# One gate-weight load in place of four, and a re-planned start, in a four-layer attention and GLU kernel

## Chip, core and metric

The kernel runs on one core of one Trainium2 chip. The metric is the device time of one execution in microseconds, lower is better. Times of a profiled execution are read from its trace, counted from the first instruction.

## What is computed

2048 tokens of width 448 pass through four residual layers: local dilated attention (A), gated bilinear MLP (B), A, B. Cut from the reference:

```python
x = A_x
x = x + _A_ref(_layernorm(x), A_wqkv, A_wo)                 # layer 0
x = x + _B_ref(_layernorm(x), B_w_gate, B_w_up, B_w_down)   # layer 1
x = x + _A_ref(_layernorm(x), A_wqkv, A_wo)                 # layer 2
x = x + _B_ref(_layernorm(x), B_w_gate, B_w_up, B_w_down)   # layer 3

def _A_ref(x, wqkv, wo):        # 16 heads of 28; each token looks at 8 tokens, 2 apart
    q, k, v = ...               # x @ wqkv
    logits = einsum("bhsd,bhswd->bhsw", q, kg) * scale
    attn = softmax(where(mask, logits, -1e9))
    return einsum("bhsw,bhswd->bhsd", attn, vg) @ wo

def _B_ref(x, w_gate, w_up, w_down):
    return einsum("bsf,fd->bsd", (x @ w_gate) * (x @ w_up), w_down)   # F = 1792
```

All data are bfloat16.

## The kernel before

Even and odd tokens are separated, so that the dilated window becomes a band of neighbours. The tokens lie in 16 blocks of 128, and each layer works on chunks of 256 or 512 tokens. `SEQ` gives the order of the jobs: `A00` is layer 0, chunk 0; `B10` layer 1, chunk 0; attention chunks and MLP chunks of the next layer alternate.

For each chunk `ln_chunk` normalises blocks on DVE and ACT (statistics `st` L582, `mv` L584, logarithm and exponential for `rstd` L585 and L587, normalised `xn_sb` L603). The normalised block is transposed into `xnTa` or `xnTb`: in layer 0, chunks 0 to 2, by TensorE against an identity (L612, copied out at L618); in all other chunks by a DMA transpose on SP's queue (L606). In layer 0 chunk 3 is blocks 10 to 13 and chunk 4 blocks 14 and 15.

Attention: `qk_chunk` multiplies by the query and key weights `WQK` (L650, four units of 14 matmuls in a chunk; a unit's key half has the key `Kps`, its query half `Qps`), evicts to `qk` (L702), and sends a few rows of it to DRAM (L711, "PW"), from where they come back transposed (L722). `v_group` makes V with `WV` (L650 too). For each block of 120 queries there are scores (L793), exponentials (L800), masks (L806), denominators (L820 early, by shuffles later) and the product with V (L826); `y_blocks` multiplies by `wo_g` (L666). MLP: `b_chunk` multiplies by gate and up weights (L907), evicts gate (L913), multiplies (L916, `hT`) and applies the down weights `WD` (L666, and L928 for the last two blocks).

The weights and x are loaded at the start, all through `plain_dma` (L464), on two queues. SP's queue has in this order: x blocks 0 to 3 (two loads), two of the four staged parts of wqkv, x blocks 4 to 7, the V weights, x blocks 8 to 11, x blocks 12 to 15, four parts of wo, and the up weights. ACT's queue has the other two staged parts, four loads of a quarter of the gate weights each, and two halves of the down weights. x, wqkv and the down weights fill 128 partitions with rows of 448 numbers or twice that. Gate weights go to partitions 0 to 63 of `WGU` and up weights to partitions 64 to 127; an up row has 1792 numbers, a row of a gate quarter 448. An instruction that issues a DMA stands in its engine's program order: on ACT it comes between activations and waits there for what it depends on.

The order on each engine is not written by hand. Every step is an `Op` with a duration, dependencies and a priority; `Sched.schedule` plays the program through with those durations and picks, engine by engine, the ready op of least priority. The loads take part with due times after their issue (`XL`, `WVL`, `STL`, `BL`, `WOL`, and the numbers called `lat`); these are planning numbers and cause no wait on the chip. Priorities come from `HEAD_P` (normalisation of the first chunks), `PR` (by kind of step) and `JP` (by job). `HOLD_BB` says how long the planner keeps a step of another matmul tiling waiting. At run time each engine follows its list and waits on semaphores for what it depends on. The list of one engine is strictly in order: an instruction that waits holds up all behind it. Before the real work TensorE runs 48 matmuls on zeros (L515).

Of the kernel before, what the change touches and what calls it, by code (L numbers as in the profile page):

```python
# [17 lines left out]
NCH = S // 512  # L18
# [8 lines left out]
MAIN = "R64"  # L27
PE_T = ('00', '01', '02')
HEAD_LN = 5
HEAD_P = (-32.97, -30.35, -18.21, -18.15, -16.4)  # L30
HOLD_A = 0.0
HOLD_BA = 2000.0
HOLD_BB = 500.0
HOLD_N = 3
D_PE = 1
DPARTS = ((0, 7), (7, 14))
# [8 lines left out]
AVC = True  # L45
AVC_E = ("act", "dve")
NBK = 8
PR = {'E': 5.21, 'lnv': 1.44, 'N': 2.25, 'S': 1.29, 'H': -17.16, 'VT': -3.79, 'QK': 2.58, 'G': 5.11, 'R': -15.24, 'Tps': 23.39, 'Ddps': -6.83, 'V': 1.75, 'Yps': -9.35, 'rstd': 0.76, 'Rs': -4.41, 'Rl': -5.78, 'mv': -8.05, 'Ex': -1.78, 'Oc': 6.12, 'QKps': -0.5, 'x': -0.56, 'Gps': 9.84, 'PW': -4.56, 'bn': 0.52, 'xn': -0.08, 'T': -7.71, 'AV': 1.69, 'VVps': 0.13}
JP = {'A04': 1.75, 'B32': 97.25, 'B33': -8.83, 'A00': -4.95, 'B12': 1.14, 'A22': 1.53, 'B10': -7.93, 'B14': 0.49, 'B13': 1.25, 'A21': -4.76, 'B11': 6.29, 'B31': 0.68, 'B34': -7.33, 'A01': -0.41, 'A23': 0.99, 'A02': 0.46, 'A20': -20.09, 'B30': 0.88, 'A03': 0.17}
XL = (2700.0, 2700.0, 5500.0, 8000.0, 10000.0)  # L50
WVL = 6500.0
STL = (3300.0, 4300.0, 3500.0, 4600.0)
BL = (9000.0, 15000.0, 12000.0)
WOL = 11000.0
PLAIN = 4
ACH = {0: (256, 512, 512, 512, 256), 2: (512, 512, 512, 512)}
BCH = {1: (256, 512, 512, 512, 256), 3: (256, 512, 512, 512, 256)}
WARM = 18
FILL = 30
SEED = 768  # L60
JITTER = 0
ATT_P = -0.09
A_CAP = 5
B_CAP = 8
SEQ = "A00 A01 B10 A02 B11 A03 A04 B12 A20 B13 A21 B14 B30 A22 B31 A23 B32 B33 B34".split()
# [339 lines left out]
def build(nc, A_x, A_wqkv, A_wo, B_w_gate, B_w_up, B_w_down, out):  # L405
# [41 lines left out]
    sc = Sched()  # L447
    LAST = sc
    sem_names = ["pe", "act", "dve", "pool"]
    sem_names += [f"d_x{i}" for i in range(NCH)] + ["d_stg0", "d_stg1", "d_stg2", "d_stg3", "d_wv", "d_wo", "d_wg0", "d_wg1", "d_wg2", "d_wg3", "d_wu", "d_wd0", "d_wd1", "d_out", "d_out2"]  # L450
    sem_names += ["d_x0h"]
    sem_names += [f"d_t{li}_{j}" for li in range(4) for j in range(len(CH[li]))]
    sem_names += [f"d_p{li}_{j}" for li in (0, 2) for j in range(len(CH[li]))] + [f"d_v{q}" for q in range(NQB)] + ["d_one0", "d_one2", "d_stv"]
# [9 lines left out]
    def plain_dma(q, dst, src, key, sem, deps=(), lat=3000.0, prio=0.0):  # L463
        sc.add(q, one(lambda E: E.dma_start(dst, src), key), {"sp": 520.0, "act": 500.0, "pool": 1000.0}[q], deps=deps, dma=sem, mode=0, lat=lat, prio=prio)  # L464
# [78 lines left out]
        src = A_wo.rearrange("(c j e) d -> j e c d", c=4, j=4, e=DH)[j]  # L543
        plain_dma("sp", dst, src, ("wo", j), "d_wo", deps=["c_wo"], lat=WOL, prio=-45)
    plain_dma("sp", WGU[64:128, :, :], B_w_up.rearrange("(k p) f -> p k f", p=64), "wu", "d_wu", lat=BL[1], prio=-44)
    for n in range(4):
        f0, f1 = n * F // 4, (n + 1) * F // 4
        plain_dma("act", WGU[0:64, :, f0:f1], B_w_gate[:, f0:f1].rearrange("(k p) f -> p k f", p=64), ("wg", n), f"d_wg{n}", lat=BL[0], deps=[("rstd", 0, 3)] * (n > 1), prio=-57 if n < 2 else -20)
    for n in range(2):
        plain_dma("act", WD[:, 7 * n:7 * n + 7, :], B_w_down[F // 2 * n:F // 2 * n + F // 2, :].rearrange("(c p) e -> p c e", p=128), ("wd", n), f"d_wd{n}", deps=[("rstd", 0, 7)], lat=BL[2], prio=-19)  # L550
    WDR = [("wd", 0), ("wd", 1)]
    WO = [("wo", j) for j in range(4)]

# [18 lines left out]
    def ln_chunk(li, j, prio):  # L572
        par = li % 2
        X = xnT[par]
        by_pe = f"{li}{j}" in PE_T
        t0, t1 = CH[li][j]
        blocks = range(t0 // 128, t1 // 128)
        groups = (1,) * len(blocks) if (li, j) == (0, 0) else (2,) * (len(blocks) // 2) + (1,) * (len(blocks) % 2)
        B0 = t0 // 128
        for n in groups:  # L580
            for B in range(B0, B0 + n):
                sc.add("dve", one(lambda E, B=B: E.bn_stats(st6[:, B, :], x_sb[:, B, :]), ("bn", li, B)), 525.0,  # L582
                       deps=[("x", li - 1, B)] + ([("xn", li - 1, B)] if li else []), prio=prio)
                sc.add("dve", one(lambda E, B=B: E.bn_aggr(mv[:, B, :], st6[:, B, :]), ("mv", li, B)), 100.0, deps=[("bn", li, B)], prio=prio - 0.1)  # L584
            sc.add("act", one(lambda E, B0=B0, n=n: E.activation(lnv[:, B0:B0 + n].unsqueeze(2), mv[:, B0:B0 + n, 1:2], ACT.Ln, bias=eps_sb[:, 0:1], scale=1.0), ("lnv", li, B0)),  # L585
                   190.0, deps=[("mv", li, B) for B in range(B0, B0 + n)] + ["c_eps"], prio=prio)
            sc.add("act", one(lambda E, B0=B0, n=n: E.activation(rstd[:, B0:B0 + n], lnv[:, B0:B0 + n], ACT.Exp, scale=-0.5), [("rstd", li, B) for B in range(B0, B0 + n)]),  # L587
                   165.0, deps=[("lnv", li, B0)], prio=prio)
            B0 += n
        for B in blocks:  # L590
            slot, prev = ring("xn", ("T", li, B) if not by_pe else ("Tps", li, B))
            if par == 0:
                src = _dup_view(x_sb[:, B, 0:256])
                dst = xn_sb[:, slot, 0:512].rearrange("p (a n) -> p a n", a=2)
                c0 = 128 * B
# [7 lines left out]
            sc.add("dve", one(lambda E, B=B, dst=dst, src=src: E.tensor_scalar(dst, src, mv[:, B, 0:1], rstd[:, B:B + 1], ALU.subtract, ALU.mult), ("xn", li, B)),  # L603
                   325.0 if par == 0 else 540.0, deps=[("rstd", li, B), ("mv", li, B), ("x", li - 1, B), prev], prio=prio - 0.2)
            if not by_pe:
                sc.add("sp", one(lambda E, slot=slot, c0=c0: E.dma_start_transpose(X[:, :, c0:c0 + 128], xn_sb[:, slot, 0:128 * nt]), ("T", li, B)),  # L606
                       1300.0, deps=[("xn", li, B)] + war, dma=f"d_t{li}_{j}", mode=0, lat=1400.0 if par == 0 else 1900.0, prio=prio)
            else:
                bk = Banks(1)
                ins = []  # L610
                for c in range(4):
                    ins.append((lambda E, c=c, slot=slot, bk=bk: E.transpose(ps[:, bk[0], :].bitcast(bf)[:, 128 * c:128 * (c + 1)], xn_sb[:, slot, 128 * c:128 * (c + 1)], ident[:]),  # L612
                                ("Tps", li, B) if c == 3 else None))
# [56 lines left out]
    def qk_chunk(li, j, prio):  # L670
# [37 lines left out]
        for b, w in [(b, w) for b in range(4) for w in range(2) if b + w < 4 and (li, j) != (0, 0)]:  # L708
            src = qk[32 * b + DH:32 * b + 32, w, :, c0:c1]
            dst = vt_dram[li].rearrange("(t w b r) n -> r w b t n", w=2, b=4, r=4)[:, w, b, :, c0:c1]  # L710
            sc.add("sp", one(lambda E, dst=dst, src=src: E.dma_start(dst, src), ("PW", li, j) if b == 3 else None), 550.0, deps=[("QK", li, j, c) for c in range(4)], dma=f"d_p{li}_{j}", mode=0, lat=3500.0 if li == 0 and j == 1 else 2200.0, prio=prio - 0.2)  # L711

    vslot, v2slot = {}, {}

    def vt_load(li, qb, prio):
        if li == 0 and qb < PLAIN:
            return
        k0, nk, _, _ = qb_info(qb)
        slot, prev = ring("v2", ("AV", li, qb))
        v2slot[(li, qb)] = slot  # L720
        deps = [("PW", li, j) for j in chunks_of(li, k0, k0 + nk)] + [("vones", li), prev]
        sc.add("sp", one(lambda E: E.dma_start_transpose(v2_sb[:, slot, :], vt_dram[li][:, k0:k0 + 128]), ("VT", li, qb)), 1300.0, deps=deps, dma=f"d_v{qb}", mode=li, lat=2500.0 if li == 0 and k0 < 768 else 1500.0, prio=prio)  # L722

    def v_group(li, qbs, prio):
        X = xnT[0]
# [161 lines left out]
    def b_chunk(li, j, n_b, prio):  # L887
# [173 lines left out]
```

## Time and profile before

| | |
|---|---|
| median of 6 runs | 406.39 us (405.11 to 407.6) |
| profiled execution | 406.44 us, its span 404.7 us, mean granted TensorE clock 0.987 |
| TensorE busy | 390.3 us (96%) |
| DVE / ACT / POOL busy | 292.7 / 222.9 / 15.5 us |
| DMA | 23.34 MB moved, 8.54 MB of it read from HBM by loads |

"Busy" is the time in which an engine had at least one instruction in work. "PE" is TensorE's matmul side, "PEld" its weight loads. A slice of the page's rows is a fortieth of the span, 10.1 us; "PEclk" is the clock that TensorE was granted, in tenths of full speed. In a view of waits a line names the engine that stood idle and what ended its idling; in a chain the pieces follow each other in time. The 1.7 us between span and time lie around the traced instructions.

### The profile page before, as it was taken

To read this page: it belongs to the slowest core of one execution; us is meant where nothing else is said; L and a number is where in the kernel's file an instruction comes from. 1 tells how busy PE (TensorE), PEld (TensorE's weight loads), DVE (VectorE), ACT (ScalarE), POOL (GpSimd) and SP (SyncE) were. 2 spreads that over 40 slices of the span, in tenths; PEclk is the share of its full clock that TensorE was granted. 3 is DMA by queue.
4 is the path that set the end of the run, shared out by engine and by line. 5 is a ranking of instruction groups with operands and counts; after the bars stand their busy time and mean duration, and the time that the engine had idled before them with its cause. 6 is when DMAs were issued, how large, how long until landed. Compare 5 with 4: busy or idle time off the path is not lost.

```text
span 404.7 us, 11727 instructions
## 1 busy us (share of the span) xinstructions
PE 390.3 (96%) x5046; PEld 212.6 (53%) x5046; DVE 292.7 (72%) x602; ACT 222.9 (55%) x406; POOL 15.5 (4%) x29
## 2 busy tenths in 40 slices
PE   8797899999999999999999999999999999999996
PEld 6443358644454444545455666844445455444584
DVE  5698398989997978687678965945784777674152
ACT  4596378676763955565564655625661575343040
POOL 6043000000000000000000000000000000000000
PEclk9899699999999999999999999999999999999999
DMA  8999141334024112222111205031030300320010
GB/s 232 271 214 213 32 59 29 62 54 64 14 47 68 33 28 46 47 28 39 15 24 25 51 16 101 20 61 43 11 45 26 70 0 3 84 55 2 13 36 24
DMA packets 58563, 23.34 MB, mean 58 GB/s; under 512 B 48112, under 2 KB 58032, under 8 KB 58512
## 3 DMA queue, kind: packets, MB, share of 16 engines
q1 hardware_dynamic: 54400, 18.86, 25.4%
q10 hardware_dynamic: 4112, 3.73, 4.0%
q8 instruction: 40, 0.66, 0.7%
q14 instruction: 11, 0.09, 0.1%
HBM read 8.54 MB, written 2.83 MB: 28 GB/s over the span
## 4 chain that ended last, share of the span: by engine, by line
PE 88%; DMA 4%; DVE 4%; ACT 1%; issue 1%; SPq 0%
PE ps L907 41%; PE ps L666 26%; PE ps L650 14%; DMA x_sb<-in_A_x_dram 2%; PE ps L826 2%; PE ps L793 2%; DMA xnTa<-xn_sb 2%; PE ps L928 1%; DVE st L582 1%; ACT E_sb L800 1%; DVE E_sb L806 1%; DVE x_sb L878 1%; PE ps L612 1%; DVE qk L702 0%; SPq L464 0%
## 5 line engine op out<-in xcount | busy, mean ns | idle before, releaser
L907 PE MATMUL ps<-xnTb,WGU 64*128 64x512 bf16 (+1 forms) x1960 | 179.4, 333 | 1.9 <-DVE R_sb L842 0.6
L907 PEld LDWEIGHTS ps<-xnTb,WGU 64*128 64x128 bf16 x1960 | 96.7, 94 | 73.0 <-issue 2.2
L913 ACT ACTIVATE g_sb<-ps 128x512 bf16<-128x512 f32 (+1 forms) x140 | 71.2, 513 | 92.7 <-PE ps L907 91.6
L916 DVE TENSOR_TENSOR hT<-g_sb,ps 128x512 bf16<-128x512 bf16 (+1 forms) x140 | 78.9, 575 | 44.8 <-ACT g_sb L913 42.1
L666 PE MATMUL ps<-WD,hT 64*128 64x448 bf16 x840 | 85.3, 349 | 0.2
L800 ACT ACTIVATE E_sb<-ps 128x960 bf16<-128x960 f32 (+1 forms) x68 | 63.0, 972 | 12.5 <-PE ps L793 12.4
L650 PE MATMUL ps<-xnTa,WQK 64*128 64x512 bf16 (+1 forms) x504 | 55.0, 362 | 5.2 <-DMA xnTa<-xn_sb 4.0
L666 PEld LDWEIGHTS ps<-WD,hT 64*128 64x128 bf16 x840 | 39.8, 94 | 37.2 <-PE ps L666 1.1
L878 DVE TENSOR_TENSOR x_sb<-x_sb,ps 128x448 bf16<-128x448 bf16 x62 | 35.9, 614 | 16.1 <-PE ps L666 16.0
L806 DVE TENSOR_TENSOR E_sb<-E_sb,MK 128x960 bf16<-128x960 bf16 (+1 forms) x64 | 43.5, 694 | 5.6 <-ACT E_sb L800 5.5
L582 DVE BATCH_NORM_STATS2 st<-x_sb 128x6 f32<-128x448 bf16 x64 | 37.3, 615 | 4.8 <-DMA x_sb<-in_A_x_dram 4.8
L650 PEld LDWEIGHTS ps<-xnTa,WQK 64*128 64x128 bf16 x504 | 24.1, 96 | 28.9 <-issue 6.5
L603 DVE TENSOR_SCALAR xn_sb<-x_sb,mv,rstd 128x512 bf16<-128x512 bf16 (+1 forms) x64 | 34.0, 573 | 1.3 <-ACT rstd L587 1.1
L666 PE MATMUL ps<-wo_g,oT 64*128 64x448 bf16 x256 | 29.6, 350 | 0.0
L702 ACT ACTIVATE qk<-ps 128x1024 bf16<-128x1024 f32 (+1 forms) x22 | 19.6, 906 | 16.6 <-PE ps L650 16.6
L702 DVE CAST qk<-ps 128x1024 bf16<-128x1024 f32 (+1 forms) x14 | 16.0, 1142 | 11.7 <-PE ps L650 11.5
L650 PE MATMUL ps<-WV,xnTa 64*128 64x336 bf16 (+2 forms) x252 | 23.9, 311 | 0.1
L844 ACT ACTIVATE R_sb<-R_sb 128x480 f32<-128x480 f32 (+1 forms) x30 | 18.0, 603 | 10.2 <-DVE R_sb L842 9.8
L860 DVE TENSOR_TENSOR oT<-O_sb,R_sb 128x480 bf16<-128x480 f32 (+3 forms) x32 | 19.5, 614 | 2.6 <-ACT R_sb L846 2.5
L846 ACT ACTIVATE R_sb<-R_sb 128x480 f32<-128x480 f32 (+1 forms) x34 | 20.4, 603 | 0.5
L842 DVE STREAM_SHUFFLE R_sb<-O_sb 128x480 f32<-128x480 f32 (+1 forms) x30 | 20.5, 689 | 0.0
L585 ACT ACTIVATE lnv<-mv,eps_sb 128x2 f32<-128x2 f32 (+1 forms) x33 | 9.6, 294 | 17.7 <-DVE mv L584 17.7
(55 smaller groups left out, 181.0 us busy)
## 6 DMA issues: line engine op xcount, KB each, us to landing
out_dram<-x_sb SPq DMA_DIRECT2D x15, 112.0 KB, 1.7
WGU<-in_B_w_gate_dram ACTq DMA_DIRECT2D x4, 392.0 KB, 10.2
WGU<-in_B_w_up_dram SPq DMA_DIRECT2D x1, 1568.0 KB, 20.3
WD<-in_B_w_down_dram ACTq DMA_DIRECT2D x2, 784.0 KB, 19.2
x_sb<-in_A_x_dram SPq DMA_DIRECT2D x3, 448.0 KB, 11.3
vt<-qk SPq DMA_DIRECT2D x49, 16.0 KB
xnTb<-xn_sb SPq DMA_TRANSPOSE x32, 3.0
v_sb<-vt SPq DMA_TRANSPOSE x30, 2.3
```

The lines of the kernel that those rows point to most:

```text
L582: sc.add("dve", one(lambda E, B=B: E.bn_stats(st6[:, B, :], x_sb[:, B, :]), ("bn", li, B)), 525.0, deps=[("x", li - 1, B)] + ([("xn", li - ...
L603: sc.add("dve", one(lambda E, B=B, dst=dst, src=src: E.tensor_scalar(dst, src, mv[:, B, 0:1], rstd[:, B:B + 1], ALU.subtract, ALU.mult), ( ...
L650: parts[0 if s < 3 else 1][1].append((lambda E, w=w, c=c, lo=lo, st=st, sp_=sp_: E.matmul(u["out"](w), u["lhs"](w, c, lo, lo + 64), u["rhs ...
L666: ins.append((lambda E, w=w, c=c, lo=lo, st=st, sp_=sp_: E.matmul(outs(w), lhs(w, c, lo), rhs(w, c, lo), start=st, stop=sp_), keys[w] if s ...
L702: return E.activation(dst, src, ACT.Copy) if hasattr(E, "activation") else E.tensor_copy(dst, src)
L800: return E.activation(E_sb[0:nk, slot, 2 * hp:2 * hp + 2, 0:4 * nq], ps[0:nk, b0:b0 + 2, 0:4 * nq], ACT.Exp, scale=SCALE)
L806: return E.tensor_tensor(e, e, m, ALU.mult)
L842: sc.add("dve", one(lambda E: E.stream_shuffle(R_sb[:, rs, 0:4 * nq], osrc(), [DH] * 32), ("Rs", li, qb)), dve_est(4 * nq) + 100.0, deps=[ ...
L878: sc.add("dve", one(lambda E: E.tensor_tensor(x_sb[:, B, :], x_sb[:, B, :], ps[:, bk[w], 0:D], ALU.add), ("x", li, B)), dve_est(D), deps=[ ...
L907: ins.append((lambda E, u=u, k=k, w=w: E.matmul(u["out"](w), WGU[64 * w:64 * w + 64, k, 128 * u["fc"]:128 * u["fc"] + 128], X[64 * w:64 * ...
L913: sc.add("act", one(lambda E, gs=gs, bk=bk: E.activation(g_sb[:, gs, 0:nt], ps[:, bk[0], 0:nt], ACT.Copy), ("G", li, j, fc)), act_est(nt), ...
L916: sc.add("dve", one(lambda E, gs=gs, bk=bk, fc=fc: E.tensor_tensor(hT[:, fc, hs, 0:nt], g_sb[:, gs, 0:nt], ps[:, bk[1], 0:nt], ALU.mult), ...
```

## The change

The four gate loads become one, with rows of 1792 numbers, issued on ACT's queue after the first key product of layer 0 instead of two at the very start and two during the head. The two down loads also wait for an eviction of chunk 1's Q/K products. The planner's due times are shortened for the later x loads, V weights, wo and the big weights, and lengthened for layer 0's DMA transposes and for two kinds of small transfers. The planner's priorities and constants are another set. `HOLD_BB` is 2000 in place of 500. The order of SP's loads is the same in both kernels.

```diff
-HEAD_P = (-32.97, -30.35, -18.21, -18.15, -16.4)
+HEAD_P = (-38.93, -34.69, -18.9, -18.15, -15.19)
-HOLD_BB = 500.0
+HOLD_BB = 2000.0
...
-PR = {'E': 5.21, 'lnv': 1.44, ...}
-JP = {'A04': 1.75, 'B32': 97.25, ...}
-XL = (2700.0, 2700.0, 5500.0, 8000.0, 10000.0)
-WVL = 6500.0
+PR = {'E': 5.39, 'lnv': 4.48, ...}
+JP = {'A04': 17.51, 'B32': 73.91, ...}
+XL = (3000.0, 3000.0, 4500.0, 5000.0, 5500.0)
+WVL = 5000.0
-BL = (9000.0, 15000.0, 12000.0)
-WOL = 11000.0
+BL = (9000.0, 13000.0, 11000.0)
+WOL = 6000.0
...
-SEED = 768
+SEED = 459
-ATT_P = -0.09
+ATT_P = 0.26
...
-    for n in range(4):
-        f0, f1 = n * F // 4, (n + 1) * F // 4
-        plain_dma("act", WGU[0:64, :, f0:f1], B_w_gate[:, f0:f1].rearrange("(k p) f -> p k f", p=64), ("wg", n), f"d_wg{n}", lat=BL[0], deps=[("rstd", 0, 3)] * (n > 1), prio=-57 if n < 2 else -20)
+    plain_dma("act", WGU[0:64, :, :], B_w_gate.rearrange("(k p) f -> p k f", p=64), "wg", "d_wg", lat=BL[0], deps=[("Kps", 0, 0, 0)], prio=-90)
     for n in range(2):
-        plain_dma("act", WD[...], ..., ("wd", n), f"d_wd{n}", deps=[("rstd", 0, 7)], lat=BL[2], prio=-19)
+        plain_dma("act", WD[...], ..., ("wd", n), f"d_wd{n}", deps=[("rstd", 0, 7), ("QK", 0, 1, 0)], lat=BL[2], prio=-19)
...
             if not by_pe:
                 sc.add("sp", ... E.dma_start_transpose(X[:, :, c0:c0 + 128], xn_sb[:, slot, 0:128 * nt]), ("T", li, B)),
-                       ... lat=1400.0 if par == 0 else 1900.0, prio=prio)
+                       ... lat=3000.0 if li == 0 else 1400.0 if par == 0 else 1900.0, prio=prio)
...
-            ("PW", li, j) ... lat=3500.0 if li == 0 and j == 1 else 2200.0
+            ("PW", li, j) ... lat=3500.0 if li == 0 and j <= 2 else 2200.0
-            ("VT", li, qb) ... lat=2500.0 if li == 0 and k0 < 768 else 1500.0
+            ("VT", li, qb) ... lat=2500.0 if li == 0 and k0 < 1024 else 1500.0
...
-            return dict(..., deps=[("wg", n) for n in range(4) if ...] + ["wu"],
+            return dict(..., deps=["wg", "wu"],
```

More of the change, by code (lines that the diff above doesn't have):

```diff
@@ L47 @@
 NBK = 8
-PR = {'E': 5.21, 'lnv': 1.44, 'N': 2.25, 'S': 1.29, 'H': -17.16, 'VT': -3.79, 'QK': 2.58, 'G': 5.11, 'R': -15.24, 'Tps': 23.39, 'Ddps': -6.83, 'V': 1.75, 'Yps': -9.35, 'rstd': 0.76, 'Rs': -4.41, 'Rl': -5.78, 'mv': -8.05, 'Ex': -1.78, 'Oc': 6.12, 'QKps': -0.5, 'x': -0.56, 'Gps': 9.84, 'PW': -4.56, 'bn': 0.52, 'xn': -0.08, 'T': -7.71, 'AV': 1.69, 'VVps': 0.13}
-JP = {'A04': 1.75, 'B32': 97.25, 'B33': -8.83, 'A00': -4.95, 'B12': 1.14, 'A22': 1.53, 'B10': -7.93, 'B14': 0.49, 'B13': 1.25, 'A21': -4.76, 'B11': 6.29, 'B31': 0.68, 'B34': -7.33, 'A01': -0.41, 'A23': 0.99, 'A02': 0.46, 'A20': -20.09, 'B30': 0.88, 'A03': 0.17}
-XL = (2700.0, 2700.0, 5500.0, 8000.0, 10000.0)
-WVL = 6500.0
+PR = {'E': 5.39, 'lnv': 4.48, 'N': 2.54, 'S': 1.51, 'H': -16.8, 'VT': 0.06, 'QK': 1.71, 'G': -2.51, 'R': -2.54, 'Tps': 24.4, 'Ddps': -3.29, 'V': 4.0, 'Yps': -16.04, 'rstd': -2.61, 'Rs': -4.21, 'Rl': -7.93, 'mv': -22.02, 'Ex': 2.02, 'Oc': 6.51, 'QKps': -1.79, 'x': -0.68, 'Gps': 21.63, 'PW': -1.17, 'bn': 1.13, 'xn': 0.26, 'T': -5.31, 'AV': 2.17, 'VVps': -0.71}
+JP = {'A04': 17.51, 'B32': 73.91, 'B33': -39.49, 'A00': -57.97, 'B12': -8.89, 'A22': 3.6, 'B10': -7.69, 'B14': -6.07, 'B13': -6.69, 'A21': -6.5, 'B11': 5.61, 'B31': 5.7, 'B34': -23.55, 'A01': -1.05, 'A23': -9.97, 'A02': -0.45, 'A20': -23.59, 'B30': 0.59, 'A03': -0.27}
+XL = (3000.0, 3000.0, 4500.0, 5000.0, 5500.0)
+WVL = 5000.0
 STL = (3300.0, 4300.0, 3500.0, 4600.0)
-BL = (9000.0, 15000.0, 12000.0)
-WOL = 11000.0
+BL = (9000.0, 13000.0, 11000.0)
+WOL = 6000.0
 PLAIN = 4
@@ L449, in build @@
     sem_names = ["pe", "act", "dve", "pool"]
-    sem_names += [f"d_x{i}" for i in range(NCH)] + ["d_stg0", "d_stg1", "d_stg2", "d_stg3", "d_wv", "d_wo", "d_wg0", "d_wg1", "d_wg2", "d_wg3", "d_wu", "d_wd0", "d_wd1", "d_out", "d_out2"]
+    sem_names += [f"d_x{i}" for i in range(NCH)] + ["d_stg0", "d_stg1", "d_stg2", "d_stg3", "d_wv", "d_wo", "d_wg", "d_wu", "d_wd0", "d_wd1", "d_out", "d_out2"]
     sem_names += ["d_x0h"]
@@ L545, in build @@
     plain_dma("sp", WGU[64:128, :, :], B_w_up.rearrange("(k p) f -> p k f", p=64), "wu", "d_wu", lat=BL[1], prio=-44)
-    for n in range(4):
-        f0, f1 = n * F // 4, (n + 1) * F // 4
-        plain_dma("act", WGU[0:64, :, f0:f1], B_w_gate[:, f0:f1].rearrange("(k p) f -> p k f", p=64), ("wg", n), f"d_wg{n}", lat=BL[0], deps=[("rstd", 0, 3)] * (n > 1), prio=-57 if n < 2 else -20)
+    plain_dma("act", WGU[0:64, :, :], B_w_gate.rearrange("(k p) f -> p k f", p=64), "wg", "d_wg", lat=BL[0], deps=[("Kps", 0, 0, 0)], prio=-90)
     for n in range(2):
-        plain_dma("act", WD[:, 7 * n:7 * n + 7, :], B_w_down[F // 2 * n:F // 2 * n + F // 2, :].rearrange("(c p) e -> p c e", p=128), ("wd", n), f"d_wd{n}", deps=[("rstd", 0, 7)], lat=BL[2], prio=-19)
+        plain_dma("act", WD[:, 7 * n:7 * n + 7, :], B_w_down[F // 2 * n:F // 2 * n + F // 2, :].rearrange("(c p) e -> p c e", p=128), ("wd", n), f"d_wd{n}", deps=[("rstd", 0, 7), ("QK", 0, 1, 0)], lat=BL[2], prio=-19)
     WDR = [("wd", 0), ("wd", 1)]
@@ L606, in ln_chunk @@
                 sc.add("sp", one(lambda E, slot=slot, c0=c0: E.dma_start_transpose(X[:, :, c0:c0 + 128], xn_sb[:, slot, 0:128 * nt]), ("T", li, B)),
-                       1300.0, deps=[("xn", li, B)] + war, dma=f"d_t{li}_{j}", mode=0, lat=1400.0 if par == 0 else 1900.0, prio=prio)
+                       1300.0, deps=[("xn", li, B)] + war, dma=f"d_t{li}_{j}", mode=0, lat=3000.0 if li == 0 else 1400.0 if par == 0 else 1900.0, prio=prio)
             else:
@@ L710, in qk_chunk @@
             dst = vt_dram[li].rearrange("(t w b r) n -> r w b t n", w=2, b=4, r=4)[:, w, b, :, c0:c1]
-            sc.add("sp", one(lambda E, dst=dst, src=src: E.dma_start(dst, src), ("PW", li, j) if b == 3 else None), 550.0, deps=[("QK", li, j, c) for c in range(4)], dma=f"d_p{li}_{j}", mode=0, lat=3500.0 if li == 0 and j == 1 else 2200.0, prio=prio - 0.2)
+            sc.add("sp", one(lambda E, dst=dst, src=src: E.dma_start(dst, src), ("PW", li, j) if b == 3 else None), 550.0, deps=[("QK", li, j, c) for c in range(4)], dma=f"d_p{li}_{j}", mode=0, lat=3500.0 if li == 0 and j <= 2 else 2200.0, prio=prio - 0.2)
     vslot, v2slot = {}, {}
@@ L721, in vt_load @@
         deps = [("PW", li, j) for j in chunks_of(li, k0, k0 + nk)] + [("vones", li), prev]
-        sc.add("sp", one(lambda E: E.dma_start_transpose(v2_sb[:, slot, :], vt_dram[li][:, k0:k0 + 128]), ("VT", li, qb)), 1300.0, deps=deps, dma=f"d_v{qb}", mode=li, lat=2500.0 if li == 0 and k0 < 768 else 1500.0, prio=prio)
+        sc.add("sp", one(lambda E: E.dma_start_transpose(v2_sb[:, slot, :], vt_dram[li][:, k0:k0 + 128]), ("VT", li, qb)), 1300.0, deps=deps, dma=f"d_v{qb}", mode=li, lat=2500.0 if li == 0 and k0 < 1024 else 1500.0, prio=prio)
     def v_group(li, qbs, prio):
@@ L898, in out @@
                 return ps[:, acq[which], 0:nt]
-            return dict(bk=acq, out=out, n=nt, deps=[("wg", n) for n in range(4) if 128 * fc < (n + 1) * F // 4 and 128 * (fc + 1) > n * F // 4] + ["wu"],
+            return dict(bk=acq, out=out, n=nt, deps=["wg", "wu"],
                         keys=(("Gps", li, j, fc), ("Ups", li, j, fc)), fc=fc)
```

## Prediction

> **What bounds the kernel now.** I read the page first, for engines and slices.
>
> ```profile
> span 404.7 us, 11727 instructions
> ...
> PE 390.3 (96%) x5046; PEld 212.6 (53%) x5046; DVE 292.7 (72%) x602; ACT 222.9 (55%) x406; POOL 15.5 (4%) x29
> ...
> PE   8797899999999999999999999999999999999996
> ...
> PEclk9899699999999999999999999999999999999999
> DMA  8999141334024112222111205031030300320010
> ```
>
> TensorE is the bound: 9 in nearly every slice. The exceptions, idle and low clock alike, lie in the first six slices (60 us), where DMA is at 8 or 9 for four. Who idles there? The waits of PE, then the chain of work up to 48 us (start, duration):
>
> ```profile
> PE ps L650 <- DMA xnTa<-xn_sb: 4.0, 1, 4.0
> PE ps L612 <- DVE xn_sb L603: 2.5, 2, 2.0
> ```
> ```profile
> 2.81 9.70 DMA x_sb<-in_A_x_dram
> ...
> 12.54 1.15 DVE st L582 x2
> ...
> 15.97 0.93 PE ps L612 x8
> ...
> 33.60 8.18 DMA xnTa<-xn_sb
> ...
> 41.92 1.46 PE ps L650 x6
> ```
>
> Two waits matter. The third x load lands at 2.81+9.70 = 12.5; statistics and transposes of its blocks follow, and PE idles 2.0 us up to 15.97. Later the DMA transposes of chunk 3 land at 33.60+8.18 = 41.8 and PE idles 4.0 us up to 41.92. What an idle stretch does afterwards is in the windows (PE, PEld, DVE, ACT, POOL busy, granted clock, DMA share, GB/s):
>
> ```profile
> 4.00:6.00 2.00, 2.00 (x11) 1.35 (x10) 1.44 (x4) 1.21 (x3) 2.00 (x3) 1.00 1.06 371
> 6.00:12.00 6.00, 5.46 (x67) 4.39 (x66) 3.15 (x11) 3.99 (x12) 0.91 (x3) 1.00 1.11 266
> 12.00:14.00 2.00, 1.97 (x37) 1.49 (x32) 1.46 (x4) 0.60 (x1) 0.00 (x0) 1.00 1.13 308
> 14.00:20.00 6.00, 4.03 (x38) 1.63 (x39) 4.71 (x17) 3.41 (x8) 0.89 (x5) 0.72 1.13 267
> 22.00:30.00 8.00, 7.91 (x120) 3.48 (x118) 7.39 (x19) 7.07 (x16) 3.85 (x2) 1.00 1.05 213
> 42.00:48.00 6.00, 6.00 (x64) 2.16 (x65) 1.10 (x2) 2.34 (x4) 0.00 (x0) 0.58 0.10 21
> ```
>
> After each idle the clock is down (0.72, 0.58). Last, the DMA issues (count, KB each, us to landing):
>
> ```profile
> WGU<-in_B_w_gate_dram ACTq DMA_DIRECT2D x4, 392.0 KB, 10.2
> WGU<-in_B_w_up_dram SPq DMA_DIRECT2D x1, 1568.0 KB, 20.3
> WD<-in_B_w_down_dram ACTq DMA_DIRECT2D x2, 784.0 KB, 19.2
> ```
>
> The up load, issued at 14.09 on SP's queue (timeline), lands at 34.4. Chunk 3's transposes, issued from 28.29 on the same queue, end 7.4 us after that.
>
> **Where the change acts.** The issue orders of the two programs say it best. SP's loads stand in the same order in both; what moves is ACT's share. TensorE's order differs only up to about 30 us; from the V products of blocks 2 to 5 on it is identical. On DVE and ACT a few neighbours are swapped later (a mask against a hidden-layer product, a statistic against an exponential). I cost those at nothing: from 70 us to 400 PE is busy in nearly every slice at 9; with that cover gone each would cost about one instruction, 0.4 to 0.7 us. The gate's split, the `lat` numbers and the constants act only through these orders.
>
> **Step 1, the head.** Two gate issues (784 KB) at 1.80 us leave the start; two more at 8.93 and 10.74 go too, and one issue waits for the first K product. Ahead of the third x load there remain x and staged wqkv. 784 KB is 0.80 MB; at 266 GB/s (the 6:12 window) 3.0 us, so it lands near 9.5 instead of 12.5. From landing to the transposes the chain takes 15.97-12.52 = 3.45 us, so they are ready near 13.0, and chunk 0's Q/K products end at 13.97 in this trace: the 2.0 us idle goes. With it goes the low clock. In the timeline:
>
> ```profile
> 16.84 1.30 PE L650 MATMUL ps<-WV,xnTa 64*128 64x448 bf16 x6
> 18.61 1.45 PE L650 MATMUL ps<-WV,xnTa 64*128 64x448 bf16 x8
> ```
>
> These 14 matmuls take 2.75 us; at 29.40 a run of 28 takes 2.50, so 14 should take 1.25: 1.5 lost. Eight transposes (0.93 against 0.62) and one score group (0.61 against 0.39) lose 0.5 more. So 2.0 + 2.0 = 4.0. The staged weights also come earlier; DVE waited 1.1 us for them (waits): 0 to 1.1, I take 0.5, since the dummy matmuls up to 9.16 cover part.
>
> Against that, the transposes of blocks 7, 8 and 9 now stand before query block 0's denominators, where blocks 8 and 9 were transposed only at 28.84, long ready. PE must wait for DVE there: 0, if DVE is ahead, to 3.45, the landing-to-transpose row; I take 1.5, because DVE was 4.71 of 6 us busy in that stretch and has the next x load's statistics to do first. Two more mode changes at about 0.1 each: 0.2. Net 4.0+0.5-1.5-0.2 = 2.8 us.
>
> The waiting gate issue holds up ACT's queue behind it: the rstd of blocks 4 and 5 and Q/K evictions. It takes 0.60 us, as two did at 8.93 and 10.74: no loss counted, 0.6 if DVE is already waiting for that rstd. The down issues now also wait for a Q/K eviction which is earlier in ACT's own order: nothing. On SP seven small copies go ahead of the transposes of chunk 4, 3.4 us by the row of 0.48 for one at 36.01; those products run near 55 us, covered by over 10.
>
> **Step 2, chunk 3's transposes.** All weights and x are 8344 KB, the page's 8.54 MB read. Without the gate the first group is 3640 KB = 3.73 MB; from 2.0 us (2:4 moved 236 GB/s, the ramp) at 371, 308 or 266 it ends at 12.0, 14.1 or 16.0. I take 308, the window with the least of the gate in it short of the best. Gate and up together are 3136 KB = 3.21 MB. Bounds: 213 GB/s, the 22:30 window, mostly the up load (upper 64 partitions alone): 15.1 us; 371: 8.7. I take 285, about the middle, since the two now write different halves in equal rows: 11.3, so up ends near 25.4 (20.7 to 31.1).
>
> A rule speaks against this. The Trainium skill, page "SBUF — State Buffer", section "Can I just issue two DMAs to hit both halves?", says that two concurrent DMAs, one at partition 0 and one at 64, were only 6% faster than one. No row here shows the pair in equal rows. By the rule 213 becomes 226 GB/s, up ends at 28.3, and the transposes land at 35.7, 0.6 later than wanted.
>
> The transposes' first issue follows PE's head: 28.29-2.8 = 25.5. The four then need 7.4 us as after 34.4 here (down weights beside them in both cases): they land at about 33 (to 38.5 with the late bound). PE wants them at 37.92-2.8 = 35.1. So the 4.0 us wait goes, and its low clock. From 41.92 to 47.4 the trace runs 6 matmuls in 1.46, two attention groups in 0.59 and 0.62, 16 matmuls in 3.25: 5.92. At the full-clock rows (12 in 1.46, 0.39, 0.38, 14 in 1.51) it is 0.73+0.39+0.38+1.73 = 3.23. Gain 4.0+2.7 = 6.7.
>
> A second rule is weaker than the rows: page "TensorE: Matmul & The Clock Gate", section "Part 1: The HAM clock gate (the "warmup" mystery)", lets the clock fall after an idle window of about 3.4 us. Here 2.0 us idle was enough for 0.72. By the rule step 1 would lose its 2.0 of low clock and the time would be 2.0 longer.
>
> **Step 3, what is late next.** With PE earlier, DVE and ACT lose the slack that the stall gave (DVE 1.10 of 6 us at 42:48, but 5.00 of 5 at 55:60). The crowded window 60:65 (DVE 4.52, ACT 4.62 of 5) lost PE 0.57 in 5 us. Over the 25 us from 35 to 60 that is 2.9 (0 to 2.9 as bounds, I take the upper).
>
> **Sum.** 2.8+6.7-2.9 = 6.6. The profiled execution took 406.44, its span 404.7; the median is 406.39, so nothing is to be scaled: 399.8 us. Best: no DVE wait, full 0.5 becoming 1.1, nothing given back: 406.4-11.6 = 394.8. Worst within the case: PE waits 3.45 in step 1, rest as taken: 401.8.
>
> **Rivals.**
> Gate and up do not overlap (the 213 bound): the transposes land at 38.5. Both gains shrink to 41.8-38.5 = 3.3, since PE waits again and the clock falls again: 403.1. For it: the 22:30 window. Against: 371 GB/s was had when both halves were written.
> The bytes decide: the same 8.54 MB keep the engines over 1.0 busy until 42, the transposes land at 41.8 again, PE only waits longer: 406.4, no change. Against: the down weights are issued some 4 us later, behind both.
> Slower: the gate's 3.5 KB rows starve the fourth x load. In DVE's new order the statistics of block 8 stand before the normalising of blocks 4 and 5, so everything stops. Beside long up rows a down half of 784 KB took 19.2 us, 42 GB/s. If all 448 KB of that load are caught, 11.0 us, plus 2.0 of low clock, less the 9.5 of steps 1 and 2: 3.5 slower, 409.9. It decides from 9.5-2.0 = 7.5 us of delay, some 310 KB left when the gate starts. Against: at 308 GB/s that load is in by 11.3 us (2800 KB), and the first Q/K unit ends near 11.5 now; 310 KB would be left only at 268 GB/s or less (2490 KB in 9.5 us), about the 6:12 rate, which had the gate in it.
>
> **How the numbers follow.** Forecast 0.66, not overlapping 0.18, bytes 0.09, starved 0.07. A difference under 0.5% (404.4 to 408.4) can't be told from none. Faster 0.82 (the first two, less a little), same 0.10, slower 0.08. The range goes from 395.5 to 404.5: the forecast's bounds and the first rival with a us beyond; the forecast's own is 395.5 to 402.
>
> **What would show it.** Right: no PE wait for x or for xnTa over 1 us before 60 us, no clock below 0.9 between 14 and 55, the query-block-4 scores some 7 us earlier, up landed by 28. Wrong: a PE wait behind DVE near 12 to 20 us with x_sb named as releaser; xnTa still named with 3 us or more; or PE losing more than 3 us between 35 and 60 to DVE or ACT.

## The result and the profile after

| | before | after |
|---|---|---|
| median, first comparison | 405.89 us | 402.7 us |
| same kernel again (e1_same_again) | 406.03 us | 403.42 us |
| profiled execution, span | 406.44, 404.7 us | 406.03, 404.3 us |

The ratio is 0.990 (95% interval 0.9885 to 0.9915), and 0.9929 (0.9903 to 0.9954) in the second comparison: 0.7 to 1.0% faster, some 3 us. The changed kernel's times spread from 398.2 to 406.0 with the mean granted clock (1.000 at 398.2 to 398.8, 0.987 at 406.0; a single run took 569.6 at 0.658), and the profiled execution lies at the slow end. The second profile of the same kernel took 404.2 (span 402.5) and shows the same course with smaller waits; where its numbers matter they are given as e1's.

The page after, in the rows that the prediction read:

```profile
span 404.3 us, 11719 instructions
...
PE 389.2 (96%) x5046; PEld 211.8 (52%) x5046; DVE 293.5 (73%) x603; ACT 223.5 (55%) x406; POOL 15.5 (4%) x28
...
PE   8994999999999999999999999999999999999996
...
PEclk9998699999999999999999999999999999999999
DMA  8999141323124112222111205131020300320010
```

The second slice of PE went from 7 to 9: the hole in the head is filled. The hole in the fourth slice (30 to 40 us) is deeper, 4 for 7, and the granted clock is still low there and behind it (8 and 6; before 9 and 6). The waits of PE and three pieces of the chain (start, duration) say what ends it:

```profile
PE ps L648 <- DMA xnTa<-xn_sb: 6.8, 2, 6.3
```
```profile
2.83 5.62 DMA x_sb<-in_A_x_dram
...
30.05 10.60 DMA xnTa<-xn_sb
...
40.79 1.47 PE ps L648 x6
```

The third x load lands at 8.45, not at 12.5. But the transposes of chunk 3, issued 3.3 us earlier than before (from 25.02), land at 40.65 instead of 41.8, and PE, which came earlier, waits 6.3 us where it waited 4.0. The windows of the same trace show the two halves of the story (PE, PEld, DVE, ACT, POOL busy, granted clock, DMA share, GB/s):

```profile
6.00:12.00 6.00, 5.86 (x75) 4.69 (x74) 5.62 (x18) 4.26 (x13) 0.97 (x3) 1.00 1.08 359
14.00:20.00 6.00, 5.32 (x82) 2.53 (x79) 5.46 (x18) 5.96 (x11) 2.54 (x5) 1.00 1.04 214
34.00:38.00 4.00, 0.51 (x6) 0.01 (x2) 3.36 (x3) 0.78 (x1) 2.06 (x2) 0.84 1.29 126
38.00:42.00 4.00, 1.21 (x6) 0.34 (x6) 0.00 (x0) 0.00 (x0) 0.00 (x0) 0.50 1.11 104
42.00:48.00 6.00, 6.00 (x66) 2.28 (x66) 1.88 (x2) 2.97 (x5) 0.00 (x0) 0.59 0.04 3
```

With the gate out of the way 6:12 moves 359 GB/s instead of 266, and 14:20 runs at full clock (0.72 before). From 34 to 42 the DMA engines are over 1.1 busy while they move only 104 to 126 GB/s (in e1 1.02 busy at 139 GB/s from 34 to 38), and TensorE stands; then come 6 us at 0.59 (0.76 in e1). The DMA issues (count, KB each, us to landing):

```profile
WGU<-in_B_w_up_dram SPq DMA_DIRECT2D x1, 1568.0 KB, 17.4
WGU<-in_B_w_gate_dram ACTq DMA_DIRECT2D x1, 1568.0 KB, 20.3
WD<-in_B_w_down_dram ACTq DMA_DIRECT2D x2, 784.0 KB, 16.1
```

Up, issued at 10.05, lands at 27.4 (34.3 before); gate, issued at 11.29, at 31.6; the down halves, issued at 21.4 and 22.0, at 36.3 and 39.3, just where they landed before (36.5 and 39.6). By the packet records gate's first bytes move only at 18 us; from about 14, when x and wo are in, to 18 up has the DMA engines all but alone, at 190 to 199 GB/s.

### The profile page after: what moved, and what is told of

Same layout as the page of the kernel before. It is cut to its first block, busy times and chain, and to the rows that moved or that the text cites. A ratio compares the mean times of both kernels' runs of the same rounds, so it can differ in the third digit from the quotient of the medians.

```text
span 404.3 us, 11719 instructions
## 1 busy us (share of the span) xinstructions
PE 389.2 (96%) x5046; PEld 211.8 (52%) x5046; DVE 293.5 (73%) x603; ACT 223.5 (55%) x406; POOL 15.5 (4%) x28
## 4 chain that ended last, share of the span: by engine, by line
PE 83%; DMA 6%; DVE 4%; ACT 4%; issue 1%; SPq 0%; DVEq 0%
PE ps L905 41%; PE ps L664 24%; PE ps L648 13%; DMA xnTa<-xn_sb 4%; PE ps L824 2%; ACT E_sb L798 2%; PE ps L791 2%; DMA x_sb<-in_A_x_dram 1%; PE ps L926 1%; DVE E_sb L804 1%; ACT qk L700 1%; DMA xnTb<-xn_sb 1%; DVE x_sb L876 1%; DVE hT L914 1%; DVE xn_sb L601 1%
## 5 line engine op out<-in xcount | busy, mean ns | idle before, releaser
L905 PE MATMUL ps<-xnTb,WGU 64*128 64x512 bf16 (+1 forms) x1960 | 179.4, 333 | 2.5 <-DVE R_sb L840 0.9
L905 PEld LDWEIGHTS ps<-xnTb,WGU 64*128 64x128 bf16 x1960 | 96.3, 94 | 74.2 <-issue 2.3
L648 PEld LDWEIGHTS ps<-xnTa,WQK 64*128 64x128 bf16 x504 | 24.0, 96 | 30.8 <-issue 8.8
L601 DVE TENSOR_SCALAR xn_sb<-x_sb,mv,rstd 128x512 bf16<-128x512 bf16 (+1 forms) x64 | 34.3, 570 | 1.0 <-ACT rstd L585 0.8
L700 ACT ACTIVATE qk<-ps 128x1024 bf16<-128x1024 f32 (+1 forms) x22 | 19.7, 906 | 17.4 <-PE ps L648 17.3
L648 PE MATMUL ps<-WV,xnTa 64*128 64x336 bf16 (+2 forms) x252 | 22.8, 301 | 0.1
L840 DVE STREAM_SHUFFLE R_sb<-O_sb 128x480 f32<-128x480 f32 (+1 forms) x30 | 20.4, 688 | 0.0
```

Source lines behind the costliest of these rows:

```text
L648: parts[0 if s < 3 else 1][1].append((lambda E, w=w, c=c, lo=lo, st=st, sp_=sp_: E.matmul(u["out"](w), u["lhs"](w, c, lo, lo + 64), u["rhs ...
L840: sc.add("dve", one(lambda E: E.stream_shuffle(R_sb[:, rs, 0:4 * nq], osrc(), [DH] * 32), ("Rs", li, qb)), dve_est(4 * nq) + 100.0, deps=[ ...
L905: ins.append((lambda E, u=u, k=k, w=w: E.matmul(u["out"](w), WGU[64 * w:64 * w + 64, k, 128 * u["fc"]:128 * u["fc"] + 128], X[64 * w:64 * ...
```

## Experiments

Three candidates for the late transposes: A, the down load beside them; B, the gate load, which starts late; C, the transposes themselves are slow. First the kernel again, as base. In the edits below, `move` takes the issues named first out of one engine's list and puts them behind a step of another list (ahead of it with `before=True`); "..." stands for lines left out.

**e1_same_again**, no edit.

> The changed kernel as it is, for a second trace and for its spread. Theory A (the down weights, running beside chunk 3's DMA transposes on the other queue, set when these land) and rival B (the gate load starts late and leaves the up load alone, so gate and up end late) both expect about 402.7 us with runs from 398 to 406, and a trace in which PE waits for xnTa between 1 and 7 us; the shorter the time, the earlier the last of the four transposes lands. Rival C (the DMA transposes are slow by themselves) expects the same.

403.42 us. Transposes landed at 35.5 to 39.3, the wait was 5.4.

**e2_down_late**, the two down issues behind an eviction of chunk 3 (issued at 44.4):

```diff
+    move([("wd", 0), ("wd", 1)], "act", "act", ("QK", 0, 3, 2))
```

> Both down loads are issued after an eviction of chunk 3's Q/K products, so after chunk 3's transposes have landed; all else as in the changed kernel. Theory A: the four transposes land at 32 to 35 us, PE waits under 1 us for xnTa, the clock stays at 1.0, 396 to 398 us. Rival B: they start only when gate and up are done (27 to 32 us), land at 36 to 38, PE waits 2 to 3 us, 399 to 401 us. Rival C: they land at 38 to 41 as before, 402 to 403 us.

402.9 us, ratio 0.9918 (0.9885 to 0.9951): no better than e1, and the 396 to 398 of theory A were missed. But the trace has changed. The view of the tile `xnTa`, 24 to 34 us, gives the time from issue to landing of chunk 3's four transposes; first in the kernel before, then after, then here:

```profile
DMA to landing us min/median/max: 7.7/9.0/10.2
```
```profile
DMA to landing us min/median/max: 8.6/10.5/11.7
```
```profile
DMA to landing us min/median/max: 2.5/4.1/5.5
```

Without the down load beside them they land at 30.8 to 32.3, and PE does not wait for them. C falls, and so does B as the cause of this wait: gate landed at 30.3 here, no earlier than in e1 (29.5). Gate still counts: the first transpose landed 0.5 us behind it, but that early PE did not have to wait. The gain went into a new wait, which the waits of this kernel cannot name ("issue"):

```profile
PE ps L905 <- issue: 4.2, 1, 4.2
```

These are layer B's first products. Their operand `xnTb` is made by two DMA transposes issued at 46.0 and 47.4; in the view of the tile `xnTb`, 44 to 54 us:

```profile
DMA to landing us min/median/max: 7.4/7.7/7.9
```

They end at 54.8, PE starts at 55.0, and the down load ran from 44.4 to 51.7. It had only moved to the next transposes.

**e3_gate_on_sp** and **e4_gate_on_pool**: the gate issue on another queue, ahead of up on SP's, or on POOL's at about the same moment.

```diff
+    op_of("wg").deps = []
+    move(["wg"], "act", "sp", "wu", before=True)
```
```diff
+    ...
+    sc.order["act"].remove(wg)
+    sc.order["pool"].insert(sc.order["pool"].index(first), wg)
```

> The one gate load is issued on SP's queue just ahead of the up load, so that the two run one after the other and never side by side. Theory A: side by side is worth 0.4 MB by 28 us (236 to 269 GB/s against about 195), so the transposes land 1 to 3 us later, PE waits 8 us or more, 404 to 406 us. Rival B: the gate load starts some 5 us earlier than in the changed kernel and the up load ends last, at 29 to 31 us; the transposes stand behind it in the same queue and land at 38 to 41, 402 to 405 us. Rival C: unchanged, 402 to 403 us.

405.75 us, ratio 0.9997 (0.9977 to 1.0017): the whole gain is gone. One queue serves gate and up one after the other:

```profile
18.00:24.00 6.00, 5.25 (x80) 2.60 (x74) 5.78 (x14) 5.08 (x11) 4.29 (x2) 1.00 1.05 207
24.00:30.00 6.00, 6.00 (x91) 2.92 (x87) 4.51 (x12) 4.44 (x9) 0.00 (x0) 1.00 1.04 199
```

Up landed at 31.7, the transposes at 40.9, and PE waited 6.3.

> The one gate load is issued on POOL's queue at the same moment (after the first key product, about 11.3 us), all else as in the changed kernel. Rival B, with the gate's late start put down to the two queues sharing something ahead of the engines (on ACT it was issued at 11.29 but moved its first bytes at about 18, when the up load was half through): on a third queue it starts by 13 to 14 us, gate and up both end by 25 to 27 instead of 27.4 and 31.6, the transposes land by 36 to 38, 398 to 401 us. Theory A: gate and up end earlier, but the down weights then stand beside the transposes all the same: 400 to 402 us. If the gate still starts at 18 us, the late start is not the queue's: 402 to 403 us.

403.34 us, ratio 0.9932 (0.9907 to 0.9958), the time of e1. Up's rate falls only at about 18 us again, so gate seems to start no earlier from POOL's queue than from ACT's.

**Where the down load meets no transposes.** e5 puts it behind layer B's first transposes, e6 between those of chunk 4 and layer B's, e8 does e5's move alone in the kernel before.

```diff
+    move([("wd", 0), ("wd", 1)], "act", "act", ("G", 1, 0, 3))    # e5, e8
+    move([("wd", 0), ("wd", 1)], "act", "act", ("R", 0, 3))       # e6
```

> Edit to the changed kernel: ScalarE's two issues of the down weights move behind its fourth gate eviction of layer B's first chunk (L911), from about 21 us to about 53 us; the first products that need the down weights run from about 78 us. Theory D (any DMA transposes that are under way together with the down load land late, and nothing else about that load costs time): chunk 3's transposes land at 31 to 33 us as in e2_down_late, no wait of TensorE for xnTa over 0.5 us; layer B's first transposes (issued at 46.0) land by 49.5 instead of 54.8, the 4.2 us before L905 go, with the low clock after them; profile run 396 to 398.5, median 396.5 to 399.5, ratio 0.980 +- 0.004. Rival E (the 4.2 us before L905 are TensorE arriving ahead of layer B's own normalisation, with or without the load): the wait stays at 3 to 4 us, median 402 to 403.5.

396.85 us, ratio 0.9786 (0.9755 to 0.9817), as theory D had it. Layer B's first transposes landed at 50.5 and 51.4, later than the 49.5 expected, but PE came only at 50.7 and its wait before L905 fell from 4.2 to 1.0, which the view puts down to `R_sb` (L840). The view of the tile `xnTb`, 44 to 54 us, against the 7.4 to 7.9 of e2:

```profile
DMA to landing us min/median/max: 4.3/4.5/4.7
```

> Edit to the changed kernel: ScalarE's two issues of the down weights move behind its copy R_sb (L844) of block 3, to about 39 us, between the transposes of chunk 3 and chunk 4 (landed by 38.2 in e2_down_late) and those of layer B's first chunk (issued at 46.0). Theory D: two loads of 0.8 MB took 7.3 us alone in e2_down_late, so they land by 46.5 and meet no transposes that TensorE waits for: within 1.5 us of e5_down_after_block10, 396 to 399.5, and a wait before L905 of under 1.5 us. If the load runs on to 48 or later, the wait before L905 is 2 us or more and the time 400 to 402. Rival E: the wait before L905 is 3 to 4 us as in e2_down_late, median 402 to 403.5.

396.67 us, ratio 0.9778 (0.9751 to 0.9805), with e5 and e10 the fastest here, and not to be told from them. Its down load ran from about 39 to 46.9; layer B's transposes, issued at 45.7 and 47.0, took as long as in e5. In the tile view the transposes of chunk 3 took this from issue to landing, and the windows show no hole up to 48 us and no low clock:

```profile
DMA to landing us min/median/max: 2.5/2.5/4.8
```
```profile
30.00:36.00 6.00, 6.00 (x84) 2.61 (x84) 5.00 (x4) 5.19 (x6) 3.28 (x2) 1.00 0.36 67
36.00:42.00 6.00, 6.00 (x92) 2.94 (x88) 5.58 (x8) 3.52 (x5) 0.74 (x1) 1.00 0.66 127
42.00:48.00 6.00, 6.00 (x102) 3.45 (x91) 5.24 (x10) 5.57 (x9) 0.00 (x0) 1.00 0.99 252
48.00:54.00 6.00, 5.02 (x119) 4.03 (x117) 5.10 (x11) 5.41 (x11) 0.00 (x0) 1.00 0.61 61
```

> Edit to the kernel before: only ScalarE's two issues of the down weights move, from 17.0 and 20.5 us to behind its fourth gate eviction of layer B's first chunk (L913), about 54 us; gate, x and plan stay. Theory D: the up load, with the queue to itself after the gate's last quarter, lands at 28 to 31 instead of 34.3, chunk 3's transposes at 32.5 to 35.5 instead of 41.8; TensorE wants them at 37.9, so its wait of 4.0 goes and most of the low clock (2.7) with it; profile run 399.5 to 402, ratio 0.985 to 0.992, about the whole change's gain from this one move. Rival E (what is gained there comes back as a wait before layer B's first products): 403.5 to 406, ratio 0.995 to 1.0.

400.46 us, ratio 0.987 (0.9843 to 0.9896): one move of two issues in the old kernel is worth at least as much as the whole change (5.4 us by the medians, against 2.6 to 3.2). Up landed at 32.7 and the transposes at 36.3, both later than expected, and PE did not wait for them. Rival E, a wait of 3 to 4 us of layer B's own, is out in all three: 0.6 to 1.0 us is left there.

**e7_gate_at_front**, for step 1: the gate's bytes ahead of x again, as one load.

```diff
+    ...
+    sc.order["act"].insert(sc.order["act"].index(op_of(("wqk", 0, 0))), wg)
```

> Edit to the changed kernel: the gate's one load (1.6 MB, long rows) is issued by ScalarE before its first weight copy, at about 1.8 us, instead of at 11.3 us. Theory S (step 1 of the prediction: the third x load waits for the bytes ahead of it): the third x load (8.45 us) lands at 12 to 14.5, TensorE waits 2 to 5 us for the transposes of blocks 4 to 7, with a low clock behind it; the transposes of chunk 3 land no earlier than 38, since the bytes are the same; profile run 405 to 409, ratio to before 1.000 to 1.008. Rival P (the head's gain came from the plan's new order of TensorE's work, not from the bytes): the third x load lands by 10 and the time stays at 402 to 404.

406.71 us, ratio 1.0023 (1.0007 to 1.0039). The third x load landed at 16.4, later than in either kernel and later than expected, when the gate load was in (15.9); from 8 to 14 us gate got 167 to 194 GB/s and SP's queue 45 to 65. A wait of PE and its window:

```profile
PE ps L610 <- DVE xn_sb L601: 8.2, 1, 8.2
```
```profile
12.00:18.00 6.00, 0.56 (x6) 0.37 (x8) 1.56 (x5) 1.26 (x4) 0.21 (x1) 0.54 1.08 269
```

TensorE's order is that of the changed kernel, and the head's gain is gone: it hangs on the bytes ahead of x. (At chunk 3 PE comes so late here that it does not wait.) What the new order is worth by itself, no run separates.

**e9_alternate, e10_alternate_gap**: gate and up in seven pieces each, in turns on SP's queue; e10 with e6's place for the down load too.

```diff
+    ...
+    wu.ins = [(lambda E, p0=p0, w=w, k=k: E.dma_start(WGU[p0:p0 + 64, k, :], w[64 * k:64 * k + 64, :]), None) for k in range(7) for p0, w in ((64, B_w_up), (0, B_w_gate))]
```

> Edit to the changed kernel: gate and up are cut into seven pieces of 64 rows x 1792 each, issued on SyncE in turns (up, gate, up, gate ...) where the up load was; ScalarE issues no gate load; the down loads stay where the change put them (about 21 us). In e6_down_in_gap a 3584-byte packet took 284 to 300 ns while the up load ran alone (12 to 18 us, 194 to 204 GB/s) and 188 to 189 ns while both halves ran (276 to 296 GB/s). Theory W (the rate hangs on both halves being written at once; this is the 285 GB/s of the prediction's step 2, missed because the gate's load began only at 18 us): 3.21 MB from 12.5 us at 285 GB/s end at 24 to 25.5 for both, the down loads at 31 to 34, chunk 3's transposes 1 to 2 us behind these, 32.5 to 35.5; TensorE's wait for xnTa 0 to 1 us, median 396.5 to 399.5. Rival O (pieces go through one queue one after the other, 195 GB/s): gate and up land at 28 to 30, the rest as in the changed kernel, wait 5 to 6.5 us, 402 to 404.

403.37 us, ratio 0.9958 (0.9932 to 0.9985): a miss for theory W. The turns raised the rate only to 242 to 247 GB/s (16 to 24 us), not to 285; up was in at 27.7 and gate at 29.7, the down load ended at 38.0, the transposes at 39.6, and PE waited 4.8. Rival O has the time and the landings, but its 195 GB/s were exceeded too.

> Edit to the changed kernel: both, gate and up in seven pieces in turns on SyncE as in e9_alternate, and the down loads at about 39 us as in e6_down_in_gap. Theory W: gate and up land at 24 to 25.5 instead of 26 to 29.2, chunk 3's transposes, issued from about 25 us, land at 28 to 31; TensorE had no wait for xnTa in e6_down_in_gap any more, so the time is that of e6 within 1 us: 396 to 397.5. Rival O: landings as in e6_down_in_gap, the same time. A time over 398 would mean that fourteen issues on SyncE hold something back that three did not.

396.68 us, ratio 0.9784 (0.973 to 0.9838), as e6. With the down load away, how gate and up are cut and queued no longer shows.

**e11_gate_quarters, e12_swap_quarters**: is it the gate's long rows or its place?

```diff
+    ...
+    wg.ins = [(lambda E, f0=f0: E.dma_start(WGU[0:64, :, f0:f0 + F // 4], B_w_gate[:, f0:f0 + F // 4].rearrange("(k p) f -> p k f", p=64)), None) for f0 in range(0, F, F // 4)]
+    sc.order["act"][i], sc.order["sp"][j] = wu, wg    # e12 alone: the queues change places
+    ...
```

> Edit to the changed kernel: the gate's one load is cut again into four loads of a quarter of the columns (rows of 448 numbers) as in the kernel before, all four issued by ScalarE where the changed kernel issues the one, from 11.3 us; all else stays. It costs ScalarE three more issues of about 0.6 us in the head. In all runs so far with a wait for chunk 3's transposes the span ends 363 us after these landed (404.7-41.8, 402.5-39.3, 402.3-39.6), so the time is 363 + landing + 1.7. Theory L (long equal rows side by side are what moved the landing by 2.5 us, from 41.8 to 39.3): beside the up load the quarters get 20 to 56 GB/s as from 22 to 30 us in the kernel before (213 GB/s in all), all loads end at about 39 to 40 again, the transposes land at 40.5 to 42.5, wait 6 to 8 us, 405 to 407, ratio 0.997 to 1.003. Rival M (the place of the gate behind x moved it, the row form does nothing): landing 38.5 to 40, wait 4 to 6 us, 402 to 404, ratio 0.990 to 0.995.

405.71 us, ratio 0.999 (0.9971 to 1.0009), but for neither reason. The timeline of ACT:

```profile
11.49 8.82 ACTq L1010 DMA_DIRECT2D WGU<-in_B_w_gate_dram  x4
20.36 0.20 ACT L585 ACTIVATE rstd<-lnv 128x2 f32<-128x2 f32 x1 [8.66 <-issue]
```

Four issues held ACT 8.8 us, where one took 0.70, and PE waited 7.5 us for ACT.

> e11_gate_quarters did not answer its question: ScalarE stood 8.8 us in its four gate issues (11.5 to 20.3), and TensorE waited 7.5 us for ScalarE. Here the queues change places, so that no engine with work stands still: SyncE issues the four gate quarters (rows of 448 numbers) where it issued the up load, and ScalarE issues the one up load (rows of 1792) where it issued the gate load, at 11.3 us. The landing of chunk 3's transposes decides, the span ends about 363 us after it. Theory L (two halves in equal long rows are what moved the landing from 41.8 to 39.3): the short rows beside the long ones bring the pair back to 200 to 255 GB/s, as in e11 from 18 to 26 us (213 to 256 against 276 to 296 in e6_down_in_gap); landing 40.5 to 42.5, time 404.5 to 407, ratio 0.996 to 1.003. Rival M (the gate's place behind x moved it, the row form does nothing): landing 38.5 to 40, time 402 to 404, ratio 0.990 to 0.995.

404.08 us, ratio 0.9943 (0.9917 to 0.997), landing 39.7, wait 4.7: rival M, by its ratio; its median is 0.1 over M's band. It is not to be told from e1 (0.9903 to 0.9954), but lies above the first comparison (0.9885 to 0.9915), so a small effect of the rows stays possible; and since the two loads also changed queues, the rows' form is not tested alone.

## Why the prediction was right, and where it was not

The time was forecast at 399.8 and is 402.7, inside the range and faster as said. That is partly luck: the forecast's own mechanism (no wait left at chunk 3) did not happen, its own band ended at 402, and the range reaches 404.5 because it took in a rival. By the sign that the prediction itself named (`xnTa` still waited for 3 us or more) it was wrong there. Its steps fared differently.

**Step 1 held.** x was to land at 9.5 and landed at 8.45; 14:20 ran at full clock; e7 shows the cause. PE came to chunk 3's need at 34.5 (40.79 less 6.28) instead of 37.92: 3.4 us, forecast 2.8; in the six traces with this head and a wait there (the first, e1, e3, e4, e9, e12) it is 2.9 to 3.8. Where nothing eats it, between e8 and e5, which have the down load at the same place, it is 3.6 (spans 399.1 and 395.5). The term sized wrongly was the 1.5 us behind DVE for the transposes of blocks 7 to 9: PE's waits for `xn_sb` (L601) are 0.7 in all in e6, against 2.5 before. The 2.0 us put on the low clock are worth less than that by themselves: e8 has the head of the kernel before without the low clock, yet starts its run of 28 V products at 29.27 instead of 29.40, because PE then waits for DVE (1.0 us in three places).

**Step 2 failed at one term: "The four then need 7.4 us as after 34.4 here (down weights beside them in both cases)".** The 7.4 was read as the price of four transposes, counted from the landing of up. It was the price of what was still under way: in the kernel before, up landed at 34.3 and the last down half 5.2 us later. After the change up landed at 27.4, inside the bounds, but gate (to 31.6) and the down load (to 39.3) were still to come, and the transposes took 13.2 us from there. They end 0.4 to 2.2 us behind the down load in all seven traces that wait for them (before, the first after, e1, e3, e4, e9, e12), wherever up and gate lie. Without it they take 2.5 to 6.1 us each (e2, e5, e6, e8, e10), and what is still under way is gate or up: the first of them lands 0.5 us behind the later of the two in all five. Then the 6.7 us of this step appear nearly whole: in e8 the first product with `wo_g` starts at 41.48 instead of 47.95, 6.5 earlier, and 5.6 are left at the end (404.7 to 399.1).

The rule weighed there does not decide it. The Trainium skill, page "SBUF — State Buffer", section "Can I just issue two DMAs to hit both halves?", gives 6% for two concurrent DMAs; in e6 the pair on two queues ran at 274 to 297 GB/s from 18 to 22 us, against 201 to 204 from 14 to 18 with up nearly alone. The measurement is far above the rule here, and still the landing hung on the down load.

**Step 3 was too dear.** Of the 2.9 us, 0.4 appeared: 48:54 in e6 has PE at 5.02 of 6, and 1.0 us is PE's wait for `R_sb` (L840), of which the kernel before already had 0.6 (60:65 in the prediction). So with the down load away the gains nearly add up: 5.6 from e8 and the 2.9 to 3.8 of step 1 are 8.5 to 9.4, and e6's span is 9.4 shorter than before's.

**The rivals.** "The bytes decide" (0.09) had the mechanism: loads and transposes share the engines, the end comes with the last of them, "PE only waits longer". It erred in calling that no change. The loads end sooner in e1, 37.7 against 39.6 (39.3 in the first trace). The head does not explain that: 6:12 moves 0.56 MB more (93 GB/s for 6 us), but 12:18 only 202 GB/s instead of 287, which gives 0.51 MB back. The lead comes where the two halves run side by side: from 18 to 30 e1 moves 265 and 243 GB/s in 6 us each, the kernel before 221 and 217. The span ends 362.9 us after the landing in before (404.7-41.8) and 363.2 in e1 (402.5-39.3), 362.0 to 363.6 in the seven traces that wait: the 2.5 us by which the landing moved in e1 are the gain (2.2 in the spans), and step 1's are lost in waiting. e3 takes the side-by-side away and lands at 40.9, with no gain; e12 keeps it with short rows and keeps most of the gain. "No overlap" (0.18) had nearly the number, 403.1, and nearly the landing, 38.5, and gate does start only at 18; but e2 and e6 start gate at about the same time and have no wait there, so that is not why. "Starved" (0.07) did not occur, but its mechanism is real: in e7 the third x load got what a gate load left it (45 to 65 GB/s, that rival's row was 42), and the time was 406.7.

## What to carry to other kernels

A time from issue to landing is the price of everything that shares the DMA engines, so before a DMA is moved, list what will still be under way at its new place. Weights that are needed late (here from 78 us, in e6 from 68) belong in a gap between transposes that TensorE waits for, not "last" in a queue that reaches into them. If a gain in front of a wait turns into a longer wait, the thing waited for sets the time, and the span minus its landing stays the same (here within 2 us).

## What the hardware showed beyond that

- DMA transposes and an ordinary load beside them slow each other: at 34:38 both together moved 126 GB/s, at a busy share of 1.29, where the down load alone moved up to 317 (e6, 42 to 44 us) and the transposes alone landed in 2.5 us. How the engines share them out is not shown.
- A load of 1.6 MB into 64 partitions ran at about 195 GB/s alone, and one issued on ACT's queue at 11.3 moved its first bytes at 18, 6.7 us after its issue. Why is not settled: from POOL's queue (e4) it began no earlier (18.4), and in e12, with gate first and in quarters, the up load on ACT's queue was the one that began late, at 16.6.
- An issue can hold its engine: four on ACT's queue behind a long load took 8.8 us (e11), while the same four on SP's queue, ahead of it, took 2.8 (e12).
- The granted clock changes in steps of 3.41 us, and the idle time inside one step decides. In the kernel before it falls at 16.30 and 40.19 us and comes back at 19.71 and 47.02; all changes in the 14 traces lie whole steps apart. 13 full-speed steps had 2.0 us or more of TensorE idling, and all were followed by half speed; the other 1580 had at most 1.4, and none was. So the 2.0 us wait of the kernel before, whole in one step, cost the clock, and the 1.9 us wait of e8, cut by the border at 14.6, did not. The step of the kernel before (PE busy for 1.40 of 3.40 us; the clock is 0.50 from 16.3 to 19.7), then that of e8 (1.99 of 3.40; the clock stays at 1.00):

```profile
12.90:16.30 3.40, 1.40 (x25) 0.95 (x21) 3.40 (x13) 1.14 (x4) 0.89 (x5) 1.00 1.15 298
```
```profile
14.60:18.00 3.40, 1.99 (x34) 1.11 (x36) 3.00 (x12) 2.39 (x8) 0.79 (x5) 1.00 1.12 269
```

  The Trainium skill, page "TensorE: Matmul & The Clock Gate", section "Part 1: The HAM clock gate (the "warmup" mystery)", lets the clock fall after an idle window of about 3.4 us. The length fits these steps, but a step need not be idle throughout: 2.0 of 3.41 us were enough.
